# A pipeline a job apart for the weight conversion beside an attention recurrence

## The chip, the cores and the metric

One core of a Trainium2 chip. The metric is the device time of one execution in microseconds (us), the median of three timed runs. One more execution was profiled; all rows below are of it.

## The reference, cut to what matters

An attention recurrence is followed by two dense layers over its output:

```
for t in range(768):                      # batch 4, heads 8, head size 40
    y[t]  = r[t] @ state
    Sa    = state @ a[t]
    state = state * w[t] - outer(Sa, b[t]) + outer(v[t], k[t])
x = y as 3072 tokens x 320
h = x @ w_in;  x = (h * sigmoid(1.702 * h)) @ w_out        # 320 -> 2048 -> 320
g = x @ w_gate;  out = (silu(g) * (x @ w_val)) @ w_out2    # 320 -> 1536 -> 320
```

Activations are float32. The five weight matrices are float64, and the chip turns them into float32 itself.

## The kernel before

**Units and slots.** The 768 steps are cut into 24 units of 32 steps (`u`), and a unit into eight slots (`i`), so that t = 8u + i runs from 0 to 191. In a manual schedule (`layer_one`) every engine takes its instructions in the order in which the program writes them. Slots 0 to 4 of a unit form a chain over PE, ACT and DVE: `g_r` (L506) and ACT's `rs`, `g_md` and `md`, `g_u` and `us`, `g_ut` and `ut`, then `g_su`, whose product DVE masks into `us` (L443). In slots 5 and 6 PE sums `psmy` (L577), and `my_close` (L603) lets DVE write the state `mt` (L608) and the outputs `x` (L613). The second `my_close` ends the unit. For each group of four units there are also preparations (`prep`: scans, L389 and L398, and products, on DVE) and a triangular solve of 31 pivots, two DVE operations each (L493, L498), and a transpose L501 that PE's `g_u` (L552) of the next group needs. The first solve stands in front of slot 0. Later ones lie in the slots t%32 = 20 to 33.

**Layer one's products.** From slot 38 on every slot ends with seven to nine steps of the first dense layer (`products`): `h_part` sums into one PSUM tile (L212), ACT makes `sg` and `gh` (L216, L218), GpSimd `gl` (L220), and `o_part` sums the result one part later. After the last unit the second dense layer loads its weights and runs (`Down`, L889 to L911), up to the end.

**Conversion.** 89 pieces of up to 128 x 256 numbers are converted. A piece is loaded by SP as pairs of 32-bit words (`cva`, 3 buffers, L79). ACT squares the high word into `cvw` (2 buffers, L87) and scales the low word in place (L89). DVE builds the float32 bits in `cvu` (1 buffer) in three operations: L99 shifts and masks the high word, L103 puts sign and top bits back, L107 sets tiny values to zero with the help of `cvw`. GpSimd adds the low word into `cvw` (L109). Then comes the piece's finish: for the first 44 pieces (`first`, 4 quarters of 11) ACT rounds the result (L120, L182, L190) and GpSimd takes the remainder (L121, L183, L191), for the other 45 (`late`) SP stores `cvw` to DRAM (L1119, L1124, L1131).

**Order of the conversion.** `chain` writes these operations into a list: load three pieces, and then for piece i: square, L99, L103, finish of piece i-1, L107, add, load of piece i+2. Each of the four quarters has a chain of its own. `convert(n)` takes n entries of the list: 3 (loads) in front of the first solve, then 7 a slot, or 2 a slot where t%32 > 19 and at t = 32, 64 and so on; for the late pieces 4 or 2. A piece is seven entries. The call stands at the slot's end, ahead of `products`. The late pieces begin when block 0 of the first layer is done, at slot 69.

Of the kernel before, what the change touches and what calls it, by code (L numbers as in the profile page):

```python
# [51 lines left out]
class Convert:  # L52
# [4 lines left out]
    def __init__(self, tc, ctx):  # L57
        self.tc = tc
        self.nc = tc.nc
        self.p = ctx.enter_context(tc.tile_pool(name="cv", bufs=1))  # L60
        self.ps = Ring(ctx, tc, "cvs", 2)
        self.p2 = Ring(ctx, tc, "cv2", 2)
        self.p3 = Ring(ctx, tc, "cv3", 3)
        self.p1 = Ring(ctx, tc, "cv1", 1)

    def piece(self, src, finish):

        nc = self.nc
        st = {}
        wide = src.dtype != F32  # L70
        rows, cw = src.shape[0], src.shape[1] // (2 if wide else 1)

        def take():
            st["w"] = self.p2.tile([128, self.CW], F32, tag="cvw", name="cvw")

        def load():
            if wide:
                a = st["a"] = self.p3.tile([128, self.CW, 2], U32, tag="cva", name="cva")
                nc.sync.dma_start(out=a[0:rows, 0:cw].rearrange("p c k -> p (c k)"), in_=src)  # L79
            else:  # L80
                take()
                nc.sync.dma_start(out=st["w"][0:rows, 0:cw], in_=src)

        def square():
            take()
            lo, hi = (st["a"][0:rows, 0:cw, k] for k in range(2))
# [4 lines left out]
        def step(i):  # L91
# [6 lines left out]
            if i == 0:  # L98
                v.tensor_scalar(  # L99
                    out=u, in0=hi, scalar1=3, scalar2=0x3FFFFFF8, op0=ALU.logical_shift_left, op1=ALU.bitwise_and  # L100
                )
            if i == 1:
                v.scalar_tensor_tensor(  # L103
                    out=u, in0=hi, scalar=0xC0000000, in1=u, op0=ALU.bitwise_and, op1=ALU.bitwise_or
                )
# [5 lines left out]
        steps = [square] + [lambda i=i: step(i) for i in range(4)] if wide else []  # L111
        return load, steps, lambda: finish(st["w"][0:rows, 0:cw])
# [13 lines left out]
    @staticmethod  # L126
    def chain(pieces):

        out = [p[0] for p in pieces[:3]]
        finish = None  # L130
        for i, (_, steps, f) in enumerate(pieces):
            if finish and not steps:
                out.append(finish)
                finish = None
            out += steps[:3]
            if finish:
                out.append(finish)
            out += steps[3:]
            if 0 < i < len(pieces) - 2:
                out.append(pieces[i + 2][0])  # L140
            finish = f
        return out + [finish]
# [526 lines left out]
def layer_one(att, dense, conv, conv_in, conv_late):  # L669

    tc, up = att.tc, att.up
    first, late = ([f for q in conv_in for f in q], list(conv_late))
    done = [0]

    def convert(n):
        for _ in range(n):
            if first:
                f = first.pop(0)
                done[0] += 1
            elif late and up.hdone > 0:  # L680
                f = late.pop(0)
            else:
                return
            if f:
                f()

    up.before = lambda q: convert(sum(len(x) for x in conv_in[:q + 1]) - done[0])
# [7 lines left out]
    with tc.manual_schedule():  # L695
# [28 lines left out]
        convert(3)  # L724
# [32 lines left out]
        for u in range(NU):  # L757
            for i in range(8):
                t = 8 * u + i
                if i == 0:  # L760
                    att.g_r(u)
                    if u + 1 < NU:
                        att.load_tok(u + 1)
# [37 lines left out]
                busy = t % 32 > 19 or t % 32 == 0 and t  # L801
                convert((2 if busy else 7) if first else (2 if busy else 4))
# [3 lines left out]
        convert(len(late))  # L806
# [139 lines left out]
def general(tc, cst, seq, w_in, w_out, w_gv, w_out2, xn, out):  # L946


    nc = tc.nc
# [4 lines left out]
    with ExitStack() as ctx:  # L954
# [61 lines left out]
        with ExitStack() as cx:  # L1016
            conv = Convert(tc, cx)

            def put(src, dst):
                load, steps, finish = conv.piece(src, lambda w: nc.vector.tensor_copy(dst, w))  # L1020
                for f in [load] + steps + [finish]:
                    f()
# [58 lines left out]
def words(t):  # L1081

    return t if t.dtype == F32 else t.bitcast(U32)


def convert_jobs(conv, up, w_out, w_gv, w_out2, in_ab, in_m, out1, gv, out2):
# [11 lines left out]
    for q in range(4):  # L1098
        p = []
# [12 lines left out]
        first.append(conv.chain(p))  # L1112
# [19 lines left out]
    return first, conv.chain(second)  # L1132
# [118 lines left out]
```

## Time and profile before

| what | value |
|---|---|
| median of 3 timed runs | 1328.28 us (1325.41 to 1332.05) |
| profiled execution | 1322.78 us, of which the span is 1320.7 us |
| PE busy | 1136.4 us (86% of the span) |
| DVE, ACT, GpSimd (POOL) busy | 625.1, 435.1, 254.0 us (47%, 33%, 19%) |
| mean granted TensorE clock | 0.97 |

PE = TensorE matmul, PEld = its weight loads, DVE = VectorE, ACT = ScalarE, POOL = GpSimd, SPq = the DMA queue of SyncE. A busy share is a mean over stages that have different limits. Units end at L613's second execution: 88.99 us for unit 0, 129.10 us for unit 1; the edges of the windows below are such ends. A bracket at the end of a timeline row is the idle time of the engine ahead of this instruction, and what ended it. A shape stands as out<-in.

### The profile page before, as it was taken

The numbers are of one execution on the slowest core, as the hardware profiler recorded it, in microseconds if no ns is written. First come the engines' busy times: TensorE is split into PE (matmuls) and PEld (weight loads), VectorE is DVE, ScalarE is ACT, GpSimd is POOL, SyncE is SP. The second block draws the span as 40 slices with busy tenths as digits, with TensorE's granted clock in tenths as the row PEclk, the third lists the DMA queues.
The fourth block names the chain that finished last, engine by engine and source line by source line (L and its number), as shares of the span: only waits on it lengthen the run. The fifth ranks groups of instructions, "written<-read, shape, count | busy, mean of one in ns | idle before, by whom it ended". The sixth has DMA issues, their size and how long they took to land.

```text
span 1320.7 us, 42940 instructions
## 1 busy us (share of the span) xinstructions
PE 1136.4 (86%) x19258; PEld 933.4 (71%) x19258; DVE 625.1 (47%) x1216; ACT 435.1 (33%) x889; POOL 254.0 (19%) x255
## 2 busy tenths in 40 slices
PE   3155566899889988998899899899999999999997
PEld 3144455677667766776677687687888888888886
DVE  6864587477535963496348400244332323232222
ACT  3133324443343344334333332355222222222221
POOL 2052314452234232322232212100000000000000
PEclk9999999989989989999899999999999999999999
DMA  6345355455564556455644522355000000000000
GB/s 186 99 126 151 99 153 168 149 164 157 168 183 137 180 171 182 137 171 168 198 137 128 183 99 63 127 179 194 26 24 20 25 20 24 21 0 20 0 21 23
DMA packets 85704, 148.10 MB, mean 112 GB/s; under 512 B 8520, under 2 KB 32840, under 8 KB 85512
## 3 DMA queue, kind: packets, MB, share of 16 engines
q1 hardware_dynamic: 85512, 145.27, 36.0%
q8 instruction: 153, 2.51, 0.8%
q14 instruction: 39, 0.32, 0.1%
HBM read 111.03 MB, written 27.66 MB: 105 GB/s over the span
## 4 chain that ended last, share of the span: by engine, by line
PE 71%; DVE 10%; DMA 7%; issue 6%; ACT 3%; POOL 2%; SPq 1%; DVEq 0%; ACTq 0%; POOLq 0%
PE gv L889 20%; PE h L212 11%; PE psmy L577 9%; PE oacc L909 3%; PE oacc L910 3%; PE oacc L911 3%; PE acc L239 3%; PE acc L241 3%; PE acc L243 3%; DMA wr<-w_gv 2%; DVE tsol L498 2%; DVE tmp L493 2%; PE psn L432 2%; PE pssv L469 1%; PE pst L452 1%
## 5 line engine op out<-in xcount | busy, mean ns | idle before, releaser
L889 PE MATMUL gv<-xst,wg 128*128 128x512 f32 x1152 | 279.9, 395 | 0.6 <-DVE xst L875 0.6
L212 PE MATMUL h<-xst,wi 120*128 120x512 f32 x768 | 230.0, 435 | 23.5 <-ACT sg L216 18.2
L889 PEld LDWEIGHTS gv<-xst,wg 128*128 128x128 f32 x1152 | 213.0, 187 | 47.1 <-DVE xst L875 1.0
L212 PEld LDWEIGHTS h<-xst,wi 120*128 120x128 f32 x768 | 149.6, 204 | 66.1 <-ACT sg L216 22.2
L893 DVE TENSOR_TENSOR sg<-gv,sg 128x512 f32<-128x512 f32 x72 | 49.8, 692 | 231.6 <-PE gv L889 231.6
L220 POOL TENSOR_TENSOR gl<-sg,gh 128x512 fp32r<-128x512 f32 x80 | 105.7, 1321 | 218.6 <-ACT gh L218 143.3
L109 POOL TENSOR_TENSOR cvw<-cvu,cva 128x256 uint32<-128x256 uint32 (+2 forms) x89 | 72.4, 814 | 234.0 <-DVE cvu L107 143.3
L216 ACT ACTIVATE sg<-h 128x512 f32<-128x512 f32 x96 | 56.9, 592 | 120.8 <-PE h L212 104.6
L892 ACT ACTIVATE sg<-gv 128x512 f32<-128x512 f32 x72 | 43.3, 601 | 152.6 <-PE gv L889 152.6
L910 PE MATMUL oacc<-wo,zh 128*128 128x320 f32 x288 | 88.9, 309 | 0.0
L909 PE MATMUL oacc<-wo,zh 128*128 128x320 f32 x288 | 88.9, 309 | 0.0
L911 PE MATMUL oacc<-wo,zl 128*128 128x320 f32 x288 | 88.5, 309 | 0.0
L895 ACT ACTIVATE zh<-sg 128x512 fp32r<-128x512 f32 x72 | 45.4, 631 | 122.5 <-DVE sg L893 122.5
L239 PE MATMUL acc<-gh,wo 128*128 128x512 f32 x192 | 82.4, 429 | 3.9 <-DMA wo<-w_out 3.9
L577 PEld LDWEIGHTS psmy<-rv,md 40*64 40x64 f32 (+1 forms) x1472 | 55.6, 136 | 39.7 <-DVE us L443 16.1
L577 PE MATMUL psmy<-rv,md 40*64 40x32 f32 (+1 forms) x1472 | 66.2, 224 | 17.9 <-DVE us L443 15.1
L241 PE MATMUL acc<-gh,wo 128*128 128x512 f32 x192 | 79.9, 416 | 0.0
L243 PE MATMUL acc<-gl,wo 128*128 128x512 f32 x192 | 77.4, 404 | 0.0
L498 DVE TENSOR_TENSOR tsol<-tsol,tmp 128x31 f32<-128x31 f32 (+15 forms) x186 | 73.4, 395 | 6.4
L493 DVE TENSOR_TENSOR tmp<-tsol,nsol 128x31 f32<-128x31 f32 (+15 forms) x186 | 73.8, 397 | 4.7
L897 DVE TENSOR_TENSOR zl<-sg,zh 128x512 fp32r<-128x512 f32 x72 | 49.8, 692 | 43.7 <-ACT zh L895 43.3
L87 ACT ACTIVATE cvw<-cva 128x256 f32<-128x256 f32 (+2 forms) x89 | 38.4, 431 | 83.2 <-DMA cva<-in_ab 22.9
(118 smaller groups left out, 1721.6 us busy)
## 6 DMA issues: line engine op xcount, KB each, us to landing
wo<-w_out SPq DMA_DIRECT2D x48, 640.0 KB
rv<-rv SPq DMA_DIRECT2D x48, 208.0 KB
cva<-out SPq DMA_DIRECT2D x35, 256.0 KB
kb<-kb SPq DMA_DIRECT2D x21, 416.0 KB
toks<-ts SPq DMA_DIRECT2D x24, 320.0 KB
tok<-toks SPq DMA_DIRECT2D x24, 320.0 KB
cva<-gv SPq DMA_DIRECT2D x30, 256.0 KB
vt<-vtok SPq DMA_DIRECT2D x24, 288.0 KB
```

Of the source, the lines that this page charges most:

```text
L212: nc.tensor.matmul(ps, self.wi[:, b, 128 * f:128 * f + 128], x[:, a], start=(i == 0), stop=(i == 7))
L220: self.sub.tensor_tensor(lo, sg, hi.bitcast(F32), op=ALU.subtract)
L239: nc.tensor.matmul(acc[i], w[:, c:c + 128], hi, start=st, stop=False)
L241: nc.tensor.matmul(acc[i], w[:, 256 + c:384 + c], hi, start=False, stop=False)
L243: nc.tensor.matmul(acc[i], w[:, c:c + 128], lo, start=False, stop=sp)
L493: nc.vector.tensor_tensor(tv, tsol[:, s:s + 1, 0:n].to_broadcast([128, m, n]), self.nsol[:, s, s + 1:32].unsqueeze(2).to_broadcast([128, m ...
L498: nc.vector.tensor_tensor(t, t, tv, op=ALU.add)
L577: self.nc.tensor.matmul(ps[64 * g:64 * g + n, q % 2, 2 * x + p, c], w[:, D * g:D * g + n], r, start=(q, g) not in first, stop=False, skip_ ...
L889: nc.tensor.matmul(ps, w[:, b], x[:, a], start=(i == 0), stop=(i == 7))
L909: nc.tensor.matmul(acc[k], hi[:, c], self.wo[:, f, 0], start=st, stop=False)
L910: nc.tensor.matmul(acc[k], hi[:, c], self.wo[:, f, 1], start=False, stop=False)
L911: nc.tensor.matmul(acc[k], lo[:, c], self.wo[:, f, 0], start=False, stop=sp)
```

## The change

`chain` now makes one list of ticks for all 44 first pieces, and one for the 45 late ones, without the break between quarters. Tick T has two halves. The first half issues the finish of piece T-4 and the add of piece T-3, the second half DVE's three operations (`words`) of piece T-2, the square of T-1 and the load of T. `convert_start`, at the slot's start, takes ticks by a credit of 0.7 a slot up to t = 31, 1 a slot from t = 32 while first pieces are left, and 0.4 a slot for the late ones; it issues the first half. `convert_end`, where `convert` stood, issues the second half. In front of the first solve stand four whole ticks in place of three loads. L103 and L107 write the high word of `cva` in place, with both words eight bytes apart; `cvu` lives from L99 to L103 alone. `cvw` has 3 buffers.

```diff
         def take():
-            st["w"] = self.p2.tile([128, self.CW], F32, tag="cvw", name="cvw")
+            st["w"] = self.p3.tile([128, self.CW], F32, tag="cvw", name="cvw")
...
-            if i == 0:
-                st["u"] = self.p1.tile([128, self.CW], U32, tag="cvu", name="cvu")
-            u, w = (st[n][0:rows, 0:cw] for n in "uw")
-            f = u.bitcast(F32)
...
-            if i == 1:
-                v.scalar_tensor_tensor(
-                    out=u, in0=hi, scalar=0xC0000000, in1=u, op0=ALU.bitwise_and, op1=ALU.bitwise_or
-                )
-            if i == 2:
-                v.scalar_tensor_tensor(out=f, in0=w, scalar=TINY * TINY, in1=f, op0=ALU.is_ge, op1=ALU.mult)
-            if i == 3:
-                nc.gpsimd.tensor_tensor(w.bitcast(U32), u, lo, op=ALU.add)
...
+            u = self.p.tile([128, self.CW], U32, tag="cvu", name="cvu")[0:rows, 0:cw]
+            w, f = st["w"][0:rows, 0:cw], hi.bitcast(F32)
+            v.tensor_scalar(
+                out=u, in0=hi, scalar1=3, scalar2=0x3FFFFFF8, op0=ALU.logical_shift_left, op1=ALU.bitwise_and
+            )
+            v.scalar_tensor_tensor(out=hi, in0=hi, scalar=0xC0000000, in1=u, op0=ALU.bitwise_and, op1=ALU.bitwise_or)
+            v.scalar_tensor_tensor(out=f, in0=w, scalar=TINY * TINY, in1=f, op0=ALU.is_ge, op1=ALU.mult)
+
+        def add():
+            if wide:
+                lo, hi = (st["a"][0:rows, 0:cw, k] for k in range(2))
+                nc.gpsimd.tensor_tensor(st["w"][0:rows, 0:cw].bitcast(U32), hi, lo, op=ALU.add)
...
     def chain(pieces):
-        out = [p[0] for p in pieces[:3]]
-        finish = None
-        for i, (_, steps, f) in enumerate(pieces):
...
+        def tick(t, parts):
+            for k in parts:
+                if 0 <= t - k < len(pieces):
+                    pieces[t - k][k]()
+
+        return [(lambda t=t: tick(t, (4, 3)), lambda t=t: tick(t, (2, 1, 0))) for t in range(len(pieces) + 4)]
...
+    def convert_start(n):
+
+        credit[0] += n
+        while credit[0] >= 1:
+            credit[0] -= 1
+            convert_end()
+            if first:
+                done[0] += 1
+                a, b = first.pop(0)
+            elif late and up.hdone > 0:
+                a, b = late.pop(0)
+            else:
+                continue
+            a()
+            rest.append(b)
+
+    def convert_end():
+        while rest:
+            rest.pop()()
...
-        convert(3)
+        convert(4)
         for f in pivots:
             f()
         end()
...
                 t = 8 * u + i
+                convert_start((0.7 if t < 32 else 1) if first else 0.4)
                 if i == 0:
                     att.g_r(u)
...
-                busy = t % 32 > 19 or t % 32 == 0 and t
-                convert((2 if busy else 7) if first else (2 if busy else 4))
+                convert_end()
                 products((9, 8, 7, 7, 9, 8, 8, 8)[i])
...
-        convert(len(late))
+        convert(len(late) + 1)
```

## Rows read from the trace of the kernel before

**Rows 1.** Windows by stage: busy us of PE, PEld, DVE, ACT, POOL (instructions); clock; DMA.
```profile
63.80:89.00 25.20, 11.74 (x456) 9.83 (x456) 18.29 (x33) 8.94 (x24) 12.84 (x14) 1.00 0.35 102
89.00:129.10 40.10, 22.13 (x729) 18.75 (x728) 20.02 (x40) 13.85 (x36) 13.90 (x17) 1.00 0.50 147
129.10:164.80 35.70, 22.07 (x728) 18.61 (x728) 20.48 (x43) 11.03 (x29) 13.12 (x16) 1.00 0.36 109
164.80:203.00 38.20, 21.30 (x664) 18.41 (x664) 33.09 (x79) 8.40 (x20) 6.97 (x8) 1.00 0.59 161
203.00:301.70 98.70, 83.81 (x2104) 66.22 (x2105) 58.71 (x110) 45.66 (x108) 49.00 (x54) 0.95 0.50 160
301.70:750.00 448.30, 408.52 (x9872) 323.08 (x9871) 268.80 (x566) 167.52 (x347) 129.73 (x118) 0.94 0.54 162
```

**Rows 2.** Chain that ended last, shares by line, 63.8 to 164.8 us.
```profile
by line: issue 21.0%; PE psmy L577 19.5%; POOL cvw L109 10.3%; DVE cvu L99 6.9%; DVE cvu L107 5.4%; DVE cvu L103 5.1%; DMA cva<-in_ab 4.0%; DVE c L389 3.6%; DVE rc L398 3.3%; PE pssv L469 2.6%; POOL cvs L121 2.1%; PE psn L432 1.7%; POOL wi 
```

**Rows 3.** Timeline of DVE, unit 1: start, length, line, names, idle before.
```profile
88.58 0.41 DVE L613 TENSOR_TENSOR x<-psmy,c 104x256 f32<-104x256 f32 x1
...
114.17 0.29 DVE L99 TENSOR_SCALAR cvu<-cva 120x256 uint32<-120x256 uint32 x1 [4.04 <-DMA cva<-in_ab]
...
116.35 1.93 DVE L99 TENSOR_SCALAR cvu<-cva 120x256 uint32<-120x256 uint32 x1 [0.90 <-POOL cvw L109]
...
118.21 0.41 DVE L443 TENSOR_TENSOR us<-pssu,cst 128x256 f32<-128x256 f32 x1
...
128.69 0.41 DVE L613 TENSOR_TENSOR x<-psmy,c 104x256 f32<-104x256 f32 x1
```

**Rows 4.** Timeline of ACT, unit 1.
```profile
97.80 0.43 ACT L87 ACTIVATE cvw<-cva 128x256 f32<-128x256 f32 x1 [2.29 <-DMA cva<-out]
...
103.09 0.43 ACT L87 ACTIVATE cvw<-cva 128x256 f32<-128x256 f32 x1 [2.11 <-DMA cva<-out]
```

**Rows 5.** Timelines around the first solve: DVE, SP's queue, ACT, PE.
```profile
38.41 0.18 DVE L493 TENSOR_TENSOR tmp<-tsol,nsol 128x31 f32<-128x31 f32 x1
...
39.33 2.35 SPq L79 DMA_DIRECT2D cva<-in_ab  x2
...
48.05 0.43 ACT L87 ACTIVATE cvw<-cva 120x256 f32<-120x256 f32 x1 [7.59 <-DMA cva<-in_ab]
...
48.39 0.41 ACT L89 ACTIVATE cva<-cva 120x256 uint32<-120x256 uint32 x1
...
63.83 1.29 PE L552 MATMUL psu<-rs,ttc 32*32 32x40 f32 x64 [24.58 <-DVE low L384]
```

**Rows 6.** Instructions on tiles cva and cvw: count, ns min/median/max, first and last start.
```profile
L89 ACT ACTIVATE cva<-cva x89: 412/424/443, 48.4 to 744.1; 128x256 uint32<-128x256 uint32 x65, 120x256 uint32<-120x256 uint32 x16, 80x256 uint32<-80x256 uint32 x8
...
L99 DVE TENSOR_SCALAR cvu<-cva x89: 250/289/1953, 67.3 to 747.0; 128x256 uint32<-128x256 uint32 x65, 120x256 uint32<-120x256 uint32 x16, 80x256 uint32<-80x256 uint32 x8
...
L103 DVE SCALAR_TENSOR_TENSOR cvu<-cva,cvu x89: 376/425/1483, 67.6 to 752.7; 128x256 uint32<-128x256 uint32 x65, 120x256 uint32<-120x256 uint32 x16, 80x256 uint32<-80x256 uint32 x8
...
L107 DVE SCALAR_TENSOR_TENSOR cvu<-cvw,cvu x89: 381/425/1346, 68.1 to 753.2; 128x256 f32<-128x256 f32 x65, 120x256 f32<-120x256 f32 x16, 80x256 f32<-80x256 f32 x8
...
L120 ACT ACTIVATE cvs<-cvw x20: 400/412/419, 92.1 to 299.7; 128x256 fp32r<-128x256 f32 x20
```

**Rows 7.** Timeline of DVE and POOL inside the second solve.
```profile
171.17 0.40 DVE L498 TENSOR_TENSOR tsol<-tsol,tmp 128x231 f32<-128x231 f32 x1
...
172.26 0.82 DVE L498 TENSOR_TENSOR tsol<-tsol,tmp 128x240 f32<-128x240 f32 x1
...
171.99 0.83 POOL L109 TENSOR_TENSOR cvw<-cvu,cva 128x256 uint32<-128x256 uint32 x1 [4.14 <-DVE cvu L107]
```

**Rows 8.** The same chain as rows 2, 203 to 301.7 us, then 301.7 to 750 us.
```profile
by line: issue 19.5%; PE psmy L577 17.8%; PE h L212 8.7%; DMA cva<-in_ab 4.8%; PE psn L432 4.3%; POOL cvw L109 3.7%; PE acc L239 3.5%; PE acc L241 2.9%; PE acc L243 2.8%; POOL gl L220 2.6%; PE pssv L469 2.3%; POOL cvs L121 2.3%; DVE ttc L50
...
by line: PE h L212 23.0%; PE psmy L577 14.3%; PE acc L239 6.0%; PE acc L241 5.7%; PE acc L243 5.3%; issue 4.9%; PE psn L432 3.6%; DMA w_gv<-cvw 2.8%; PE acc L235 2.7%; PE pst L452 2.7%; PE acc L234 2.6%; PE pssv L469 2.1%; PE psu L552 2.1%;
```

**Rows 9.** ACT's waits from 330 to 760 us: total, times, longest.
```profile
ACT cvw L87 <- DMA w_gv<-cvw: 15.1, 6, 6.1
```

More of the change, by code (lines that the diff above doesn't have):

```diff
@@ L79, in load @@
                 nc.sync.dma_start(out=a[0:rows, 0:cw].rearrange("p c k -> p (c k)"), in_=src)
-            else:
-                take()
-                nc.sync.dma_start(out=st["w"][0:rows, 0:cw], in_=src)
         def square():
             take()
+            if not wide:
+                nc.sync.dma_start(out=st["w"][0:rows, 0:cw], in_=src)
+                return
             lo, hi = (st["a"][0:rows, 0:cw, k] for k in range(2))
@@ L89, in square, with words @@
             nc.scalar.activation(out=lo, in_=lo, func=ACTF.Copy, scale=2.0 ** -29)
-        def step(i):
+        def words():
+            if not wide:
+                return
             v = nc.vector
             lo, hi = (st["a"][0:rows, 0:cw, k] for k in range(2))
-            if i == 0:
-                st["u"] = self.p1.tile([128, self.CW], U32, tag="cvu", name="cvu")
-            u, w = (st[n][0:rows, 0:cw] for n in "uw")
-            f = u.bitcast(F32)
-            if i == 0:
-                v.tensor_scalar(
-                    out=u, in0=hi, scalar1=3, scalar2=0x3FFFFFF8, op0=ALU.logical_shift_left, op1=ALU.bitwise_and
-                )
-            if i == 1:
-                v.scalar_tensor_tensor(
-                    out=u, in0=hi, scalar=0xC0000000, in1=u, op0=ALU.bitwise_and, op1=ALU.bitwise_or
-                )
-            if i == 2:
-                v.scalar_tensor_tensor(out=f, in0=w, scalar=TINY * TINY, in1=f, op0=ALU.is_ge, op1=ALU.mult)
-            if i == 3:
-                nc.gpsimd.tensor_tensor(w.bitcast(U32), u, lo, op=ALU.add)
-        steps = [square] + [lambda i=i: step(i) for i in range(4)] if wide else []
-        return load, steps, lambda: finish(st["w"][0:rows, 0:cw])
+            u = self.p.tile([128, self.CW], U32, tag="cvu", name="cvu")[0:rows, 0:cw]
[9 more added lines that the diff above has]
+                nc.gpsimd.tensor_tensor(st["w"][0:rows, 0:cw].bitcast(U32), hi, lo, op=ALU.add)
+        return load, square, words, add, lambda: finish(st["w"][0:rows, 0:cw])
     def split_out(self, w, view, *dst):
@@ L127, in chain @@
     def chain(pieces):
-        out = [p[0] for p in pieces[:3]]
-        finish = None
-        for i, (_, steps, f) in enumerate(pieces):
[L132 to L142, printed above, removed]
+        def tick(t, parts):
[3 more added lines that the diff above has]
+        return [(lambda t=t: tick(t, (4, 3)), lambda t=t: tick(t, (2, 1, 0))) for t in range(len(pieces) + 4)]
 class Up:
@@ L666, in bad_flag, with layer_one @@
         nc.vector.tensor_scalar(out=bad, in0=q, scalar1=0.5, scalar2=None, op0=ALU.is_lt)
-def layer_one(att, dense, conv, conv_in, conv_late):
+def layer_one(att, dense, conv, first, part, late):
     tc, up = att.tc, att.up
-    first, late = ([f for q in conv_in for f in q], list(conv_late))
-    done = [0]
-    def convert(n):
[L676 to L687, printed above, removed]
+    done, credit, rest = [0], [0], []
+    def convert_start(n):
[15 more added lines that the diff above has]
+            rest.pop()()
+    def convert(n):
+        convert_start(n)
+        convert_end()
+    up.before = lambda q: convert(max(part * (q + 1) + 4 - done[0], 0))
     def products(n):
@@ L1019, in put @@
             def put(src, dst):
-                load, steps, finish = conv.piece(src, lambda w: nc.vector.tensor_copy(dst, w))
-                for f in [load] + steps + [finish]:
+                for f in conv.piece(src, lambda w: nc.vector.tensor_copy(dst, w)):
                     f()
@@ L1098, in convert_jobs @@
     for q in range(4):
-        p = []
+        p = first
         for g in (q, q + 4):
@@ L1111, in convert_jobs @@
         p.append(conv.piece(out1[q, 4], lambda w, d=d: conv.split_out(w, rest, *d)))
-        first.append(conv.chain(p))
     def store_gv(w, v, q, k):
@@ L1131, in convert_jobs @@
             second.append(conv.piece(out2[i], lambda w, i=i: nc.sync.dma_start(out=flat[i], in_=w)))
-    return first, conv.chain(second)
+    return conv.chain(first), len(first) // 4, conv.chain(second)
 def build(tc, consts, wd, kb, at, rv, vtok, r, k, v, w, a, b, moe_w_in, moe_w_out, in_ab, in_m, out1, gv, out2, out):
```

3 lines of the change are left out of this document (1 added, 2 removed).

## The prediction, made blind

> **What bounds the kernel now.** I read the busy shares first: PE is busy for 86% of the span, but not evenly, so I cut the span into stages with windows. In units 0 to 2 (63.8 to 164.8 us) PE works for 55.9 us of 101.0 and DVE for 58.8, and neither is full. In the second solve DVE is, with 33.1 of 38.2 us. From 203 us on PE fills: 83.8 of 98.7 us, then 408.5 of 448.3 [rows 1]. The last piece's L103 starts at 752.7 [rows 6]. So the change can win in units 0 to 2, less in the stage after them, and little later.
>
> Next I read the chain that ended last, over units 0 to 2. Conversion lines stand in it with POOL's L109 (10.3%), DVE's L99, L107 and L103 (6.9, 5.4, 5.1%), the load of `cva` (4.0%) and L121 (2.1%): 33.8% of 101 us, or 34 us [rows 2]. So for a third of this stage attention waits for conversion. The timelines show how. Unit 1 lasts 40.1 us. ACT's square L87 waits 2.29 and 2.11 us for a load, with `md` and `us` queued behind it [rows 4]. DVE's L99 stands 4.04 us for the first load of the second quarter, then another L99 waits 0.90 us for the add of the piece ahead of it and is itself stretched to 1.93 us; `us` comes behind both, at 118.21 us, and PE's `psmy` needs it [rows 3]. These five places alone are 11.0 us of the unit (2.29 + 2.11 + 4.04 + 0.90, and 1.93 less a usual 0.29).
>
> **The change part by part, in us of span.**
>
> *Units 0 to 2: -26.* A tick puts load, square, words, add and finish a tick apart, so the releaser of each is issued one tick earlier, about 1.4 slots. The whole 34 us can't come back: of 20 pieces that went into slots 0 to 19, 14 remain, and their DVE part still stands ahead of attention's instructions in DVE's queue. A piece is 0.29 + 0.43 + 0.43 = 1.14 us by the medians [rows 6], 14 of them 16 us, of which a part falls into the 42 us in which DVE now idles. So the gain lies between 34 - 16 = 18 (all of it in the way) and 34 (all of it hidden); the outer bound is 42, all of DVE's idle time. I take the middle of 18 and 34, 26; the 11.0 found in unit 1, which is 40 of the 101 us, fits that. What is late next is attention's own chain of PE, ACT and DVE.
>
> *In front of the first solve: +12.4.* This is the part that speaks against the change. Before, three loads stood there, which DVE does not wait for; pivots began at 38.41 us. The first load was issued at 39.33 and ACT's wait for it ended at 48.05 [rows 5]. Four ticks put the words of pieces 0 and 1 ahead of the first pivot in DVE's queue. L99 of piece 0 can't start before 48.05, and L103, which now writes into `cva`, must wait until ACT has read the tile, 48.39 + 0.41 = 48.80 at the latest. L103 and L107 then end at about 49.7, piece 1 adds 1.14, and pivots start near 50.8: 12.4 later. Behind them are the transpose and PE's L552, which already waits 24.58 us for DVE [rows 5], so nothing hides it. Lower bound 11 (L103 not held), upper 14 (the first add runs beside piece 1's words). SP's fourth load waits for that add, with loads behind it that unit 1 needs much later: 0.
>
> *The second solve: +6.* Slots 20 to 33 held 33 entries, 4.7 pieces; now 0.7 x 12 + 2 = 10.4 ticks. The 5.7 more pieces cost DVE 1.14 each. Besides, each has two POOL instructions; a pivot operation that met L109 took 0.82 where its neighbour took 0.40 [rows 7], so 2 x 0.42. That is 5.7 x 1.98 = 11.3, less the 5.1 that DVE idles in this window [rows 1]: 6. Bounds 0 (all falls into waits for PE) and 11. The Trainium skill (SBUF — State Buffer, Who interferes with whom) has GpSimd and a DVE operation with two SBUF inputs exclude each other for a whole instruction. By that rule, with L109's whole 0.83 in place of 0.42, this term would be about 11 and the sum 5 higher; the trace agrees that they block, and shows the smaller price in the one meeting read here.
>
> *203 to 301.7 us: -8.* In the chain stand the load of `cva` (4.8%), L109 (3.7%) and L121 (2.3%): 10.8% of 98.7, or 10.7 us [rows 8]. Ticks come once a slot here, as pieces did, with no break between quarters. PE is busy for 85% of it, so I take 8, bounds 3 and 11.
>
> *Late pieces: -3.* ACT's square waited 15.1 us in 6 places for the store of the piece whose `cvw` it takes [rows 9], and this store is 2.8% of the chain from 301.7 to 750 us, 12.6 us [rows 8]. One more buffer helps, but finish and square now stand in one slot, where it was one slot or two; SP's queue, which runs ahead, decides. I take half of 12.6 as gained, -6. Against it, in the three late solves 13 slots x 0.4 in place of 2/7 make 1.5 more pieces each, 1.5 x 1.98 x 3 = 9 us of DVE, of which PE's full queue hides two thirds: +3. The last tick falls at slot 191, beside a PE that needs nothing from it: 0. Bounds of both together -12 and +9.
>
> *In place: 0.* The trace has no DVE write with a stride of two words. Its nearest rows: L103, which reads `hi` with that stride, has the median 425 ns, L107 without any 425; ACT's L89, strided on both sides, 424 against L120's 412 [rows 6]. So 0 to +0.012 x 2 a piece. Freeing `cvu` is part of the gains above. Second dense layer, `products` and all other instructions: unchanged, 0.
>
> The sum: 12.4 - 26 + 6 - 8 - 3 = -18.6. The span goes from 1320.7 to 1302.1, the profiled execution (2.1 outside the span) from 1322.8 to 1304.2. The median of the timed runs is 5.5 above the profiled execution, so I forecast **1310 us** for it.
>
> **The rivals.**
>
> *Gain without the price (chance 0.18).* The loads ahead of the solve land earlier than ACT's wait shows, or units 0 to 2 give back most of their upper bound. Without the 12.4 us the sum is -31, with 34 in place of 26 it is -27: 1297 to 1301; with both, 1289. Against it: the queue in front of that load is the same.
>
> *The gain is eaten (0.17).* Units 0 to 2 give 18, the solve costs 11, the late pieces nothing: 12.4 - 18 + 11 - 8 = -3, 1325. For it: DVE is nearly full in the solve and has more to do there.
>
> *Slower: the square waits for the store (0.15).* Finish and square stand in one tick on one buffer. If SP is held (by a store of `toks` or a load that waits for PE) until the slot begins, ACT waits in the square for a store's landing, with the next `sg` behind it. The average such wait was 15.1/6 = 2.5 us [rows 9]. There are 42 late pieces whose square reuses a late buffer. With 6 more of them that reach PE the -18.6 is down to -4; from about 8 on there is no gain, and from 10 on the kernel is slower by over 0.5%. With 20 of them the time is 1310 + 50 = 1360. Against it: of 45 squares six waited so far, and the third buffer gives a tick, 2.5 slots, in which the add is done before the store is due.
>
> **How the numbers follow.** My own case has 0.50 and runs from 1298 to 1321 by its bounds. A measurement of this kernel tells about 0.5%, 6.6 us, from no change: faster below 1321.6, slower above 1334.9. My case and the first rival are faster: 0.68; the second rival is the same: 0.17; the third slower: 0.15. The range leaves out the far slow case and the end of the first rival: 1287 to 1332.
>
> **What would show it.** DVE idle from about 38.4 to 48 us and pivots that end some 12 us later show the price; pivots at 38.4 again refute it. Units 0 to 2 should take about 75 us in place of 101, with L99's waits for L109 gone and `us` and `md` no longer behind L87's waits. The second solve should be longer, with more pivots stretched. L103 and L107 should keep 425 ns at the median; far more refutes the zero. Late, L87's waits for `w_gv` tell the third rival: under 15 us in total for my case, over 40 for the rival. The forecast fails if the first half of a tick holds ACT or POOL in units 0 to 2, so that they stay above 90 us, or if the late stage moves by more than 10.

## The result: slower by 1.2%

The changed kernel has the median 1347.16 us (1339.71 to 1348.19, four runs) beside 1330.16 us (1325.41 to 1333.42, four runs) for the kernel before: a ratio of 1.0117, 95% interval 1.0082 to 1.0153, which is 15.6 us more. (The ratio is taken over all runs; the two medians alone differ by 17.0.) The forecast was 1310. The profiled execution of the changed kernel took 1346.77 us with a span of 1345.0 us, at its median; that of before lay some 7 us below its own. So some 7 to 9 of the 24.3 us between the two spans belong to the choice of the executions, and the ratios decide on sizes below.

In the changed kernel L85 is the square, L96, L99 and L100 are the words, L105 the add, L115/L116 (and L171/L172, L179/L180) the finishes, L77 the load, L482/L487 the pivots, L490 their transpose `ttc`, L541 `psu`, L1117 to L1129 the stores of the late pieces.

Windows of the changed kernel with the columns of [rows 1], cut at the same unit ends: end of unit 0, 1, 2, of the second solve, of units 6 and 20.

```profile
74.38:93.50 19.12, 11.68 (x456) 9.86 (x456) 15.80 (x26) 6.45 (x18) 10.62 (x12) 1.00 0.37 105
93.50:124.50 31.00, 22.04 (x729) 18.63 (x728) 16.76 (x32) 11.37 (x30) 10.43 (x12) 1.00 0.56 169
124.50:154.10 29.60, 22.05 (x728) 18.72 (x728) 19.12 (x42) 10.76 (x28) 10.88 (x14) 1.00 0.36 109
154.10:200.60 46.50, 21.09 (x664) 18.26 (x664) 41.78 (x95) 13.78 (x35) 15.95 (x18) 1.00 0.55 168
200.60:300.80 100.20, 86.88 (x2104) 68.60 (x2105) 54.55 (x106) 44.05 (x103) 45.38 (x52) 0.90 0.52 159
300.80:774.20 473.40, 415.97 (x9874) 327.92 (x9872) 258.37 (x546) 163.37 (x333) 112.39 (x109) 0.92 0.49 147
```

Against [rows 1], and against the terms of the sum:

| stage | before | after | difference | forecast |
|---|---|---|---|---|
| up to the first `psu` | 63.8 | 74.4 | +10.6 | +12.4 |
| units 0 to 2 | 101.0 | 79.7 | -21.3 | -26 |
| second solve | 38.2 | 46.5 | +8.3 | +6 |
| from there to the end of unit 6 | 98.7 | 100.2 | +1.5 | -8 |
| units 7 to 20, late pieces | 448.8 | 473.4 | +24.6 | -3 |

(In [rows 1] the last window of before ends at 750.0; its unit 20 ends at 750.5.) At the end of unit 6 the two kernels are level (301.7 and 300.8): what units 0 to 2 win is spent by then. The late pieces lose on top of it. Of the 24.6 us there, PE is idle for 17.7 more, and 7.0 more go into the same matmuls at a lower mean granted clock (0.92 for 0.94). The loss is not a matter of more work in this stage: at 0.4 ticks a slot, only 37 of the 45 late pieces reach DVE in it, where all 45 did before.

The front, as [rows 5] shows it for before: timelines of DVE, ACT and PE in the changed kernel.

```profile
46.20 0.30 DVE L96 TENSOR_SCALAR cvu<-cva 120x256 uint32<-120x256 uint32 x1 [8.89 <-DMA cva<-in_ab]
...
46.67 0.43 DVE L99 SCALAR_TENSOR_TENSOR cva<-cva,cvu 120x256 uint32<-120x256 uint32 x1 [0.17 <-ACT cvw L85]
...
48.96 0.18 DVE L482 TENSOR_TENSOR tmp<-tsol,nsol 128x31 f32<-128x31 f32 x1
46.20 0.44 ACT L85 ACTIVATE cvw<-cva 120x256 f32<-120x256 f32 x1 [10.29 <-DMA cva<-in_ab]
74.38 1.29 PE L541 MATMUL psu<-rs,ttc 32*32 32x40 f32 x64 [36.31 <-DVE low L373]
```

DVE stands 8.89 us in front of the first words, the first pivot moves from 38.41 to 48.96, and `psu` follows it by the same 10.55 us.

The late stage: ACT's waits in the square from 330 to 857 us (total, times, longest), then SP's queue and PE in the same window. For before, [rows 9] shows the row of `w_gv`, 15.1 us; the last line below adds its row of `w_out` (330 to 760 us).

```profile
ACT cvw L85 <- DMA w_gv<-cvw: 33.1, 11, 6.6
ACT cvw L85 <- issue: 10.4, 3, 6.9
ACT cvw L85 <- DMA w_out<-cvw: 4.9, 3, 3.0
SPq L77 <- POOL cvw L105: 102.6, 19, 13.0
PE h L201 <- ACT sg L205: 21.4, 8, 6.9
PE psu L541 <- DVE ttc L490: 6.8, 3, 5.1
...
ACT cvw L87 <- DMA w_out<-cvw: 5.9, 4, 2.7
```

The square now waits 38.0 us in 14 places for a store, and 10.4 in 3 places for which the trace names no releaser: 48.4 us in 17 places, beside 21.0 in 10 before. SP's loads stand 102.6 us behind the add. PE waits 21.4 us for `sg`, which stands behind the square in ACT's queue; before it waited 9.2 us there. One of these places, in the timelines of SP's queue, ACT and PE:

```profile
461.60 1.50 SPq L352 DMA_DIRECT2D rv<-rv  x2
463.55 0.43 SPq L1117 DMA_DIRECT2D w_gv<-cvw  x1
468.59 0.43 ACT L85 ACTIVATE cvw<-cva 128x256 f32<-128x256 f32 x1 [6.94 <-issue]
469.57 0.58 ACT L205 ACTIVATE sg<-h 128x512 f32<-128x512 f32 x1
470.21 0.50 PE L201 MATMUL h<-xst,wi 120*128 120x512 f32 x1 [0.39 <-ACT sg L205]
```

The store L1117 is issued late, after SP's load of `rv`. The square, for whose wait of 6.94 us the trace names no releaser, starts 5.04 us after the store's issue, and `sg` and PE's `h` follow it; PE itself stands idle for 0.39 us here. This looks exactly like the third rival. The experiments show that it is at most a part.

### The profile page after: what moved, and what is told of

The parts are those of the page before. It is cut to its first block, busy times and chain, and to the rows that moved or that the text cites. A ratio compares the mean times of both kernels' runs of the same rounds, so it can differ in the third digit from the quotient of the medians.

```text
span 1345.0 us, 42843 instructions
## 1 busy us (share of the span) xinstructions
PE 1147.1 (85%) x19258; PEld 941.4 (70%) x19258; DVE 620.9 (46%) x1216; ACT 434.9 (32%) x889; POOL 239.2 (18%) x255
## 4 chain that ended last, share of the span: by engine, by line
PE 71%; DVE 12%; DMA 6%; issue 5%; ACT 3%; SPq 2%; POOL 1%; DVEq 0%; ACTq 0%; POOLq 0%
PE gv L889 20%; PE h L201 12%; PE psmy L566 9%; DVE tsol L487 3%; PE oacc L909 3%; PE oacc L910 3%; PE oacc L911 3%; DVE tmp L482 3%; PE acc L228 3%; PE acc L230 3%; PE acc L232 3%; PE psn L421 2%; DMA cva<-in_ab 2%; PE acc L224 1%; PE pst L441 1%
## 5 line engine op out<-in xcount | busy, mean ns | idle before, releaser
L201 PE MATMUL h<-xst,wi 120*128 120x512 f32 x768 | 235.0, 442 | 35.2 <-ACT sg L205 30.2
L85 ACT ACTIVATE cvw<-cva 128x256 f32<-128x256 f32 (+2 forms) x89 | 38.5, 432 | 149.7 <-DMA cva<-in_ab 33.8
L105 POOL TENSOR_TENSOR cvw<-cva 128x256 uint32<-128x256 uint32 (+2 forms) x89 | 64.2, 722 | 89.2 <-DVE cva L100 53.3
L487 DVE TENSOR_TENSOR tsol<-tsol,tmp 128x31 f32<-128x31 f32 (+15 forms) x186 | 75.6, 406 | 6.4
L482 DVE TENSOR_TENSOR tmp<-tsol,nsol 128x31 f32<-128x31 f32 (+15 forms) x186 | 73.4, 394 | 4.9
L541 PE MATMUL psu<-rs,ttc 32*32 32x40 f32 x1536 | 22.8, 218 | 56.9 <-DVE low L373 36.3
```

The lines of the kernel that those rows point to most:

```text
L201: nc.tensor.matmul(ps, self.wi[:, b, 128 * f:128 * f + 128], x[:, a], start=(i == 0), stop=(i == 7))
L482: nc.vector.tensor_tensor(tv, tsol[:, s:s + 1, 0:n].to_broadcast([128, m, n]), self.nsol[:, s, s + 1:32].unsqueeze(2).to_broadcast([128, m ...
L487: nc.vector.tensor_tensor(t, t, tv, op=ALU.add)
```

## The experiments

Theories for the late loss: **A**, the square waits for the store of its own tick's finish (the third rival); **B**, a load waits on SP's queue for the add of its own tick and holds the stores and loads behind it; **C**, the even pace of 0.4 ticks a slot puts more work into the slots of the solves (before it was 2 entries there and 4 elsewhere); **D**, the place of a tick's first half, at the slot's start; **E**, a whole piece's work falls into one slot, where the list spread it over two to four. Ratios are to the kernel before, run on the same chip, with 95% intervals; they are formed from the single runs and are not quotients of the medians. The runs fall into three groups on three chips (up to e9, e10 to e13, e14 to e16), and runs of different groups are compared by their ratios. The diffs show the lines that matter; flags and helper functions that carry them are left out. The names e1 to e16 stand for the kernels in the expectations too.

### Two ticks ahead of the first solve (e1)

```diff
-        convert(4)
+        convert(2)
```

> The changed kernel with two ticks in front of the first solve in place of four, so that no words of DVE stand there. If the words in front of the solve cost what the trace of the changed kernel shows (DVE idle for 8.89 us, pivots 11.7 us later), the time falls by 9 to 12 us, to about 1336, and PE's first psu starts near 63.8 us again. Rival: the two pieces converted there are missed later, in units 0 to 3, and only 0 to 4 us are left. The late stage (unit 8 on) must stay within 3 us of the changed kernel's 529.

Measured: 1337.94 us, 1.0063 (1.0033 to 1.0093). PE's `psu` is back at 61.94 us:

```profile
61.94 1.29 PE L541 MATMUL psu<-rs,ttc 32*32 32x40 f32 x64 [24.58 <-DVE low L373]
...
287.30:763.70 476.40, 422.22 (x9874) 333.15 (x9872) 254.12 (x546) 162.04 (x332) 116.31 (x112) 0.90 0.49 147
```

Unit 7 ends at 314.1 instead of 327.7, so the price of the front is real in the trace; timed it is 0.5%, some 7 us, with intervals that overlap. (The expectation's 11.7 us for the pivots should be 10.55, and its last condition failed: from unit 8 on the trace has 539.6 us, 10 more than the changed kernel's 529.3, most of it after unit 20.) But with the price gone the kernel is still slower than before, and the late stage, in the second row (windows), is as long as in the changed kernel.

### Five buffers for the late `cvw` (e2)

```diff
+            if late:
+                self.count += 1
+                if self.count % 5 >= 3:
+                    st["w"] = self.ps.tile([128, 512], F32R, tag="cvs", name="cvs")[:, 0:256].bitcast(F32)
+                    return
             st["w"] = self.p3.tile([128, self.CW], F32, tag="cvw", name="cvw")
```

> The changed kernel, but late pieces take cvw from five buffers (three cvw and the two cvs, which nothing else uses then), so that the square no longer needs a buffer whose store is issued in the same tick. Theory A (the square waits for the store): ACT's waits in the square from 330 us on fall from 53 us to under 10, and the late stage from 529 us by 15 to 22, the time to about 1328. Theory B (the load waits on SP's queue for the add of its own tick, and holds what stands behind it) and theory C (the even pace puts more conversion beside the solves): no change within 4 us.

Measured: 1342.06 us, 1.0106 (1.0075 to 1.0138). Waits of ACT and PE from 330 us on:

```profile
ACT cvw L92 <- DMA cva<-gv: 0.5, 1, 0.5
...
PE psu L548 <- DVE ttc L497: 12.8, 3, 6.2
```

The square's 48 us of waits are gone, and the time hardly moves. A as the one cause falls. What comes up is PE's wait for the transpose at the end of a solve, 12.8 us in place of 6.8: DVE is late next, which is C's place.

### Five buffers for the late `cva` (e3)

The same edit for `cva` instead of `cvw`:

```diff
+                if late and self.count % 5 >= 3:
+                    a = self.ps.tile([128, 512], F32R, tag="cvs", name="cvs").bitcast(U32)
+                    a = st["a"] = a.rearrange("p (c k) -> p c k", k=2)
```

> The changed kernel, but late pieces take cva from five buffers (three cva and the two cvs), so that the load no longer waits for the add of its own tick. Theory B: SP's waits in the load, 102.6 us in 19 places, go to under 20, and the late stage falls by 10 to 20 us. Theory A: stores may come a little earlier because SP is less held, 0 to 6 us. Theory C: no change within 4 us.

Measured: 1345.3 us, 1.0108 (1.0067 to 1.015). Its profiled execution took 1357.43 us, 12 above the median, so I take from it only which waits exist: SP's loads no longer wait for the add, the square's waits stay (for `w_gv` 31.5 us in 8 places). The 102.6 us on SP's queue cost nothing that the interval, 0.4% to either side, lets show.

### The old pace for the late ticks (e4)

```diff
-                convert_start((0.7 if t < 32 else 1) if first else 0.4)
+                convert_start((0.7 if t < 32 else 1) if first else (2 / 7 if t % 32 > 19 or t % 32 == 0 else 4 / 7))
```

> The changed kernel with the late ticks at the pace of the kernel before (4/7 a slot, 2/7 where t%32 is over 19 or zero). Theory C: the late stage falls by 10 us or more, since the solves are again beside less conversion and units 20 to 23 have none. Theory A: more ticks a slot outside the solves give the stores less time, so the late stage stays within 5 us or grows, with the waits in the square still over 40 us.

Measured: 1344.28 us, 1.012 (1.0089 to 1.015). The waits of the solve are smaller, those of the square larger:

```profile
ACT cvw L85 <- DMA w_gv<-cvw: 33.6, 15, 6.2
ACT cvw L85 <- DMA w_out<-cvw: 26.3, 5, 11.8
...
PE psu L541 <- DVE ttc L490: 3.2, 2, 2.1
```

So C alone gives nothing either: with ticks closer together the square meets its store more often (59.9 us in 20 places, where it was 38.0 in 14). It may be that A and C each stand behind the other; the next experiment takes both away.

### Both together, and two ticks in front (e6)

The edits of the first, second and fourth experiment in one kernel.

> The changed kernel with three things undone: two ticks in front of the first solve, late cvw from five buffers, late pace 4/7 and 2/7 of a tick a slot. If the late loss of 25 us is the square's wait (A) and the even pace (C) together, the late stage comes back to 504 to 512 us, and with the 11 us in front the time is about 1315, ratio to the kernel before 0.985 to 0.995. If a third cause holds most of it (each of A and C alone gave back only 6 to 9 us in one profile and under 2 us in the timed runs), the late stage stays above 515 us and the time above 1328.

Measured: 1327.31 us, 0.9962 (0.9936 to 0.9989). Beside two ticks alone (1.0063) the two late edits, of which neither did anything that shows alone, give 1.0%. (Alone they were run with four ticks in front; that this makes no difference to them is assumed.)

### The kernel before, with the words in place (e7)

```diff
-                    out=u, in0=hi, scalar=0xC0000000, in1=u, op0=ALU.bitwise_and, op1=ALU.bitwise_or
+                    out=hi, in0=hi, scalar=0xC0000000, in1=u, op0=ALU.bitwise_and, op1=ALU.bitwise_or
...
-                nc.gpsimd.tensor_tensor(w.bitcast(U32), u, lo, op=ALU.add)
+                nc.gpsimd.tensor_tensor(w.bitcast(U32), hi, lo, op=ALU.add)
```

(L107 writes `hi` as well.)

> The kernel before with one part of the change alone: L103 and L107 write the high word in place, and the add reads both words from cva. My account: no change within 3 us, DVE's operations at 425 ns, the add at about 0.61 us as in the changed kernel in place of 0.74. Rival: writing with a stride makes DVE or the add meet more often, and a part of the late 25 us shows here.

Measured: 1320.99 us, 0.993 (0.9907 to 0.9953): the edit that I costed at nothing gives 9 us. The add in this kernel and in the kernel before (count, ns min/median/max), then DVE's wait in the kernel before, 60 to 302 us, which this kernel doesn't have:

```profile
L109 POOL TENSOR_TENSOR cvw<-cva x89: 604/612/1648, 68.7 to 755.6; 128x256 uint32<-128x256 uint32 x65, 120x256 uint32<-120x256 uint32 x16, 80x256 uint32<-80x256 uint32 x8
...
L109 POOL TENSOR_TENSOR cvw<-cvu,cva x89: 724/737/1752, 68.7 to 753.8; 128x256 uint32<-128x256 uint32 x65, 120x256 uint32<-120x256 uint32 x16, 80x256 uint32<-80x256 uint32 x8
```

```profile
DVE cvu L99 <- POOL cvw L109: 20.9, 25, 1.9
```

With one `cvu`, L99 had to wait until GpSimd had read the words of the piece ahead; now DVE itself frees `cvu` with L103. L103 in its turn now waits for ACT, which still reads the piece that it overwrites: 11.5 us in 9 places of the same window. And the add, with both words from one tile, takes 612 in place of 737 ns. Units 0 to 2 take 94.2 us by this alone, against 101.0.

### First pieces in ticks, late pieces by the old list (e8)

Two ticks in front; the late pieces in the order, the list and the pace of before, with three `cvw`, in place.

```diff
-        convert(4)
+        convert(2)
...
+                if not first:
+                    convert_late(2 if t % 32 > 19 or t % 32 == 0 else 4)
```

> The pipeline for the 44 first pieces alone, with two ticks in front of the solve; the 45 late pieces go by the list, order and pace of the kernel before (with words in place and three cvw). If the late pipeline is what costs, the late stage is 504 us within 4, unit 7 ends near 314 us, and the time is about 1316, ratio 0.99. If the late stage is still above 515 us, the cause is not in the order of the late conversion but in something that both share (in place, the buffers).

Measured: 1317.5 us, 0.9894 (0.9856 to 0.9932), the fastest version together with one of the next two. Windows of units 3 to 6 and 7 to 20:

```profile
140.60:287.40 146.80, 108.63 (x2768) 87.37 (x2769) 99.00 (x206) 59.95 (x144) 62.67 (x73) 0.95 0.54 163
287.40:741.10 453.70, 411.87 (x9873) 326.07 (x9871) 267.59 (x567) 167.42 (x347) 125.57 (x119) 0.94 0.54 161
```

The late stage is 453.7 us, as in the in-place kernel (456.1). From this kernel to the one with two ticks in front only the late pieces differ: 0.9894 to 1.0063, 1.7% or 22.5 us. That is the late loss without the scatter of single executions.

### Late ticks at the slot's end, and more first pieces ahead of the second solve (e9, e13)

The first of these moves both halves of a late tick to where `convert_end` stands, in the kernel with both late edits and two ticks in front, e6. The second is e8 with more ticks ahead of the solve: 18 in place of 15 pieces are begun on DVE ahead of unit 3.

```diff
                 convert_end()
+                if late_now:
+                    convert(2 / 7 if t % 32 > 19 or t % 32 == 0 else 4 / 7)
```

```diff
+                convert_start((0.9 if t < 20 else 0.35 if t < 33 else 1) if first else 0.4)
```

> As the first kernel of this call, but for late pieces both halves of a tick stand at the slot's end, so that no add and no store stands ahead of attention's instructions. If the place of the first half (the add at the slot's start, ahead of attention on GpSimd and of the next gl) is the third cause, this is faster than that kernel by 8 us or more; if not, the same within 4 us.

> e8 with the first pieces at 0.9 a slot up to slot 19 and 0.35 in slots 20 to 32, so that the second solve has some five pieces fewer beside it. By my prediction's term the solve (units 3 and 4, 65.3 us in e8) falls by 5 to 8 us; units 0 to 2 get four pieces more and lose 2 to 5. Sum 0 to -5 us: ratio 0.985 to 0.990. If DVE's work is in the way in units 0 to 2 as well, no gain.

Measured: 1323.74 us, 0.9969 (0.9942 to 0.9995), against 0.9962: D falls. And 1315.49 us, 0.9896 (0.9854 to 0.9938), against 0.9894: units 3 and 4 take 59.1 in place of 65.3 us, and units 0 to 2 end at 146.3 in place of 140.6. Work moved out of the solve is paid in the units ahead of it.

### Four and four buffers; five `cvw` at the even pace (e10, e12)

Two ticks in front in both. The first gives the late pieces four `cva` and four `cvw` at the old pace, the second five `cvw` at 0.4.

```diff
+                if late and self.na % 4 == 0:
+                    a = self.ps.tile([128, 512], F32R, tag="cvs", name="cvs").bitcast(U32)
...
+                if self.nw % 4 == 0:
+                    st["w"] = self.ps.tile([128, 512], F32R, tag="cvs", name="cvs")[:, 0:256].bitcast(F32)
```

> Two ticks in front, late pace 4/7 and 2/7, and late cva and cvw from four buffers each, so that neither the square nor the load needs a buffer that is freed in its own tick. e6 had five cvw and three cva and was at 0.9962; e8, with the list for the late pieces, at 0.9894. Theory B (the load that waits on SP's queue for the add of its own tick) as what is left: SP's waits in the load go from 32 us to under 5 and the ratio to 0.987 to 0.992. Theory E (a tick puts a whole piece's work into one slot, where the list spread it over two to four): 0.994 to 0.999, as e6.

> e6 with the even pace of 0.4 a slot put back, so this and e6 differ in the pace alone. Theory C (the even pace, worth something once the square doesn't wait): 1.002 to 1.008, with PE's waits for the solve's transpose at 8 us or more. If the pace is worth nothing, 0.9962 within 0.003.

Measured: 1333.12 us, 1.0007 (0.9973 to 1.004), with no wait of a load for an add left (75.6 us in e6, 32.4 of them for adds in `cvw` and 43.2 in the two borrowed buffers), and no better than e6 with its five `cvw` (0.9962): B falls. And 1332.07 us, 1.0031 (1.0005 to 1.0057): the even pace costs 0.7% once the square's waits are away (0.9962 to 1.0031), and the square's waits 0.3% at the even pace (1.0063 to 1.0031), which the intervals don't tell from nothing.

The traces show where the pace reaches PE. The chain that ended last over units 7 to 20, shares by line, in the changed kernel, in e12 and in e6:

```profile
by line: PE h L201 17.3%; PE psmy L566 13.1%; issue 6.2%; DVE tsol L487 5.3%; DVE tmp L482 4.9%; PE acc L228 4.4%; PE acc L230 4.2%; PE acc L232 4.0%; PE psn L421 3.3%; DMA w_gv<-cvw 3.0%; PE acc L224 2.1%; PE acc L223 1.9%; PE pssv L458 1.
...
by line: PE h L208 21.4%; PE psmy L573 14.1%; issue 6.0%; PE acc L235 5.7%; PE acc L237 5.5%; PE acc L239 5.1%; DVE tsol L494 3.7%; PE psn L428 3.4%; DVE tmp L489 2.8%; DMA x2s<-o 2.6%; PE acc L231 2.6%; PE acc L230 2.5%; PE pssu L465 2.0%;
...
by line: PE h L208 23.0%; PE psmy L573 14.1%; PE acc L235 6.7%; PE acc L237 6.4%; PE acc L239 5.9%; issue 4.9%; PE psn L428 3.4%; PE acc L231 3.0%; PE acc L230 2.8%; DMA x2s<-o 2.4%; PE pssu L465 2.2%; PE psr L510 2.2%; PE psr L519 2.1%; PE
```

The solve's pivots (`tsol`, `tmp`) are 10.2% of it in the changed kernel and 6.5% in e12, which has the even pace too. In e6, and before the change [rows 8], they are not among the lines named, all of 2.1% or more. With the even pace DVE finishes the late solves so late that attention waits for their pivots.

### Late ticks entry by entry (e11, e15)

The order of the ticks, cut into single instructions and taken as the old list was, 4 or 2 a slot, with five `cvw`; then with four and four buffers.

```diff
+        for t in range(len(pieces) + 4):
+            for k in (4, 3, 2, 1, 0):
+                if 0 <= t - k < len(pieces):
+                    f = pieces[t - k][k]
+                    out += [lambda i=i, f=f: f(i) for i in range(3)] if k == 2 else [f]
```

> Late pieces in the order of the ticks and with five cvw and three cva, but taken entry by entry (seven a tick, 4 or 2 a slot at its end) as the list was. Theory E: as e8, 0.987 to 0.992. Theory B: the load still waits for the add of its own tick, so as e6, 0.994 to 0.999.

> e11 (order of the ticks, taken by entries; 0.9945) with cva and cvw from four buffers each, so that no load or square needs a buffer freed in its own tick. If lumps and the load's wait together are what is left: 0.987 to 0.992, as e8. If the order of the ticks costs by itself: 0.993 to 0.998.

Measured: 1324.68 us, 0.9945 (0.9912 to 0.9978), and 1323.5 us, 0.9946 (0.9917 to 0.9975). Between them and the old list (0.9894) some 0.5% are left for the ticks' order and buffers, with intervals that overlap.

### The fastest version with lumps, and with an even pace (e14, e16)

Both are the kernel with the late list. The first saves up its entries and issues seven at a time, a whole piece; the second issues 2.8 entries in every slot, on the average.

```diff
+                    lump[0] += 2 if t % 32 > 19 or t % 32 == 0 else 4
+                    if lump[0] >= 7:
+                        lump[0] -= 7
+                        convert_late(7)
```

```diff
+                    lump[0] += 2.8
+                    convert_late(int(lump[0]))
+                    lump[0] -= int(lump[0])
```

> e8 (0.9894) with the list of the late pieces taken seven entries at a time, a piece's worth in one slot, at the same mean pace. Theory E (a piece's whole work in one slot is what costs, whatever its order): 0.994 to 1.000. If order or buffers are what is left between e8 and e6: 0.986 to 0.992.

> e8 with the late list at the even pace, 2.8 entries a slot everywhere in place of 4 and 2. Theory C (the even pace puts more conversion beside the solves and beside units 20 to 23): 0.995 to 1.000, the late stage up by 6 to 12 us. If the pace only matters for whole ticks: 0.987 to 0.992.

Measured: 1330.66 us, 1.0006 (0.9981 to 1.0032), and 1328.62 us, 1.0001 (0.9968 to 1.0033). Each takes back the whole 1.1% that the version with the list gains, without a tick, an added buffer or a changed order. So each of lumps (E) and even pace (C) suffices to cost 1.1% here. The stage is 466.5 and 461.4 us long, against 453.7. The even pace of 2.8 entries is also below the list's mean of 3.2, so that conversion goes on past unit 20; the units from 21 on are no longer for it (83.0 us for 84.8).

That a lump costs as much in the ticks doesn't follow. DVE's waits in the list's kernels from 330 to 857 us, with lumps, at the even pace and in e8:

```profile
DVE cva L101 <- ACT cvw L85: 32.8, 12, 6.6
...
DVE cva L101 <- ACT cvw L85: 32.6, 6, 11.1
...
DVE cva L101 <- ACT cvw L85: 12.1, 4, 5.4
```

L101 overwrites what ACT's square of the same piece reads, and a lump puts both into one slot. A tick has its square one tick ahead; the changed kernel has 11.7 us of this wait, in 2 places. So lumps in the list may be paid by a wait that the ticks have less of, and no run tells how much of the changed kernel's loss is the lumps'; cutting its ticks into entries gave back 0.2% (e6 to e11), less than the intervals.

How a wait grows is seen at the even pace in windows of 4 us over the end of unit 9 and the start of unit 10, which begins at 388.8, and in e8 below it, where unit 10 begins at 385.1:

```profile
376.00:380.00 4.00, 3.25 (x95) 2.56 (x93) 1.54 (x2) 1.19 (x3) 1.83 (x2) 1.00 0.80 250
380.00:384.00 4.00, 3.17 (x50) 2.17 (x52) 2.05 (x5) 0.21 (x1) 0.00 (x0) 0.81 0.03 5
384.00:388.00 4.00, 4.00 (x127) 3.56 (x112) 0.42 (x1) 1.02 (x2) 0.00 (x0) 0.50 0.08 13
388.00:392.00 4.00, 4.00 (x48) 2.77 (x52) 1.76 (x4) 0.00 (x0) 1.85 (x2) 0.50 0.98 297
...
396.00:400.00 4.00, 1.87 (x63) 1.54 (x53) 3.87 (x7) 1.12 (x3) 0.67 (x1) 0.95 0.03 12
400.00:404.00 4.00, 4.00 (x18) 3.27 (x17) 0.37 (x2) 1.01 (x2) 1.85 (x2) 0.63 0.00 0
```

```profile
376.00:380.00 4.00, 4.00 (x104) 3.31 (x103) 3.77 (x6) 1.04 (x3) 2.66 (x2) 1.00 0.85 244
380.00:384.00 4.00, 3.81 (x147) 3.00 (x148) 1.34 (x3) 1.23 (x2) 1.88 (x2) 1.00 0.16 61
384.00:388.00 4.00, 3.41 (x144) 2.58 (x134) 2.05 (x5) 0.00 (x0) 0.00 (x0) 1.00 0.76 217
388.00:392.00 4.00, 3.71 (x168) 2.88 (x144) 2.81 (x5) 1.99 (x6) 0.80 (x2) 1.00 0.64 185
```

At the even pace PE idles 1.6 us in the first 8 us, and in the next 8 it is full at a granted clock of 0.50, the 1.2 GHz level; after a further 2.1 us of idle time the mean of a window falls to 0.63. The kernel with the old pace idles 0.2 us in the first 8 and 0.9 in the next 8, and stays at 1.00 (earlier in unit 9 it falls too, and the mean of that unit is 0.83 there and 0.77 at the even pace). Unit 10 takes 35.7 us at the even pace and 31.0 with the old one, the largest difference of any unit in this stage.

## Why the prediction was wrong

**The front, +12.4: right.** The term measured +10.6. Of its steps, the load was there 1.85 us earlier than I took from ACT's wait before (46.20 for 48.05); the write in place does wait for ACT, for 0.17 us, and begins 0.47 us after the first of the words, where I had allowed 0.75.

**Units 0 to 2, -26: right in sign and size (-21.3), its cause only in part.** DVE's waits for the add are gone, as forecast. But 6.8 of the 21.3 come without any ticks, from the words in place (101.0 to 94.2 in e7).

**In place, 0: wrong.** The durations of L103 and L107 did stay. Tile statistics of the changed kernel, for [rows 6]:

```profile
L99 DVE SCALAR_TENSOR_TENSOR cva<-cva,cvu x89: 422/427/1465, 46.7 to 833.8; 128x256 uint32<-128x256 uint32 x65, 120x256 uint32<-120x256 uint32 x16, 80x256 uint32<-80x256 uint32 x8
L100 DVE SCALAR_TENSOR_TENSOR cva<-cvw,cva x89: 422/427/1532, 47.1 to 834.2; 128x256 f32<-128x256 f32 x65, 120x256 f32<-120x256 f32 x16, 80x256 f32<-80x256 f32 x8
```

The medians are 427 ns for 425. What I left out is who frees `cvu`, which I had put down to the ticks, and that the add reads other tiles. Alone it is worth 9 us in the timed runs.

**The second solve, +6: +8.3, right, in part by luck.** I had 11.3 us of work and meetings, less 5.1 of DVE's idle time that they would fill. DVE's work grows by 8.7, of which the pivots' longer times are 2.2 where I had 4.8, and its idle time falls by 0.4 alone, to 4.7. The two errors cancel. DVE is busy for 41.8 of 46.5 us. In the timeline 21 pivot operations of this window overlap a GpSimd instruction, before it was 9. One such place:

```profile
163.47 0.40 DVE L482 TENSOR_TENSOR tmp<-tsol,nsol 128x240 f32<-128x240 f32 x1
163.91 0.70 DVE L487 TENSOR_TENSOR tsol<-tsol,tmp 128x240 f32<-128x240 f32 x1
163.64 0.71 POOL L105 TENSOR_TENSOR cvw<-cva 128x256 uint32<-128x256 uint32 x1 [3.63 <-DVE cva L100]
```

The pivot beside the add is 0.30 longer than its neighbour. The Trainium skill (SBUF — State Buffer, Who interferes with whom) has the later one wait until the other instruction has ended; the trace agrees that they block, with 0.30 us of price here for an add of 0.71 that had 0.44 left when the pivot began. In [rows 7] it is 0.42 us, for an add that had 0.56 left: in both places what was left of the add, less 0.14.

**203 to 301.7 us, -8: wrong, +1.5.** I took the chain's rows of load, add and finish as gain. The load of `cva`, part of that gain, is still in the chain, with 6.6% of 100.2 us where it had 4.8% of 98.7. And with the ticks four pieces fewer are begun on DVE ahead of unit 3 (17 for 21), and DVE has 96.3 us of work in units 3 to 6 in place of 91.8. These units take 146.7 us, 136.9 before, 138.2 with the words in place alone, and 146.8 in the fastest version. Nearly half of what units 0 to 2 win is lost again there: of 21.3 us 11.5 are kept (21.3 less 9.8).

**Late pieces, -3, bounds -12 and +9: this step failed, and it decides the result.** It is about +25 us in the two traces, +22.5 by the runs that differ in the late pieces alone. I named the square's wait as the one price and gave the case 0.15. The test that I wrote down, the square's waits for `w_gv` under 15 us for my case and over 40 for the rival, gave neither: 33.1, and 48.4 only with `w_out` and the waits without a named releaser. And the waits were not the cause by themselves: without them the time stayed (1.0106 for 1.0117). I had costed the pace at 9 us of DVE's work in the solves, "of which PE's full queue hides two thirds"; but the pace costs 0.7% in the ticks without the square's waits (0.9962 to 1.0031, some 9 us), and in the list the pace and the lumps cost 1.1% each (0.9894 to 1.0001 and 1.0006). So PE's queue, at 408.5 of 448.3 us [rows 1], hides the list at four and two entries a slot. It doesn't hide seven entries at once, nor 40% more of them in the slots of a solve, where the chain then runs through the pivots.

The steps from the late ticks to the old list, in per cent of the time of before: the square's waits 0.3, the pace 0.7, entry by entry 0.2, the old order and buffers 0.5; the sum is the 1.7 of the runs. No step but the pace is clearly larger than its interval, and in another order they have other sizes (nothing for the first two alone with four ticks in front). The whole of the 15.6 us: -9.3 in place, -4.8 the first pieces in ticks with two in front, +22.5 the late ticks, +7.2 two more ticks in front. The second and the last have overlapping intervals. My own case's 1298 to 1321 was also too narrow by its own terms: their bounds, added up, run from 46 us less to 13 more, which is 1282 to 1341.

Open is the path by which the lumps reach PE, and what PE waits for in the gaps of units 9 and 10 above: the trace names no releaser for them. The square's waits and the lumps, as parts of the late loss, are not told from nothing. Whether the ticks' order itself costs the 0.5% is open too, and how the 9 us in place divide between the freed `cvu` and the shorter add.

## What to carry to other kernels

A pipeline whose steps are a job apart pays where its engines wait for each other, which is in a stage whose bound engine is idle; in a stage that is nearly full, spread the same work thin, keep it out of the slots that are already crowded, and leave its pace uneven where the load is. When two causes cover each other, taking one away may show nothing: try them together before either is called harmless. And count for every buffer which engine frees it: here that, with a shorter add, was worth 9 us; the pipeline of the first pieces in its better form gave some 5 more, which its interval doesn't tell from nothing.

## What the runs showed of the hardware

The same matmuls of the late stage (some 9,870) take 408.5 us of PE's busy time at a mean granted clock of 0.94 and 422.2 at 0.90 (e1). In units 9 and 10 above, at the even pace, PE idled for 1.6 us and later for 2.1, and each time a stretch below full clock followed, down to 0.50 and 0.63.

GpSimd's add of two 128x256 words takes 612 ns with both from one tile, each read with a step of eight bytes, and 737 ns with one of them from a tile of its own, read without a step.

Loads that stood 102.6 us in all on SP's queue behind the add cost nothing that the intervals show: 1.0117 with these waits, 1.0108 without them.
